# Crossbar transposes for more heads of an attention kernel, with three staging buffers and two crossbar targets

## The chip, the cores and the metric

The kernel runs on one core of one Trainium2 chip. The metric is the device time of one execution in microseconds; the profile's span, from the first to the last instruction, is a little shorter. Three runs of the kernel before took 318.65 to 319.55 us, with a median of 319.01 us.

## The reference

There are two stages. The first is attention over 8 batches, 8 heads, 576 positions and a head dimension of 64. The first four heads see a plain causal window of 32 positions, the last four every fourth position of a causal window of 128:

```python
scores = scale * np.matmul(q, k.transpose(0, 1, 3, 2))
mask_plain = (rel >= 0) & (rel < window)                       # window 32
mask_dil = (rel >= 0) & (rel < window * dilation) & (rel % dilation == 0)   # dilation 4
attn = softmax(where(mask, scores, -1e9))                      # written shorter here
x = (attn @ v), heads side by side: 4608 tokens of 512 features
h = np.maximum(x @ w_in, 0.0)
out = h * h @ w_out
```

The second stage is a feed-forward block with a hidden width of 2048 on the 4608 tokens. Inputs and output are 32-bit floats; the kernel computes in bf16.

## The kernel before, in words

**Two interleaved streams.** TensorE runs the feed-forward block in groups: tiles of 512 tokens (the first four of 256), each of 16 or 8 groups of first-layer matmuls (line 529; the Relu is on ScalarE at line 540, the square on VectorE at line 541) and 16 or 8 groups of second-layer matmuls (line 561). Between the groups stand the steps of the attention of later batches, so that a batch's rows of xT are ready when the feed-forward block reaches them. The schedule is manual: each engine runs its instructions in the order in which the program names them, and waits on semaphores where data or a buffer is not ready.

**The order** is written out in the string PROGRAM for batches 0 to 4 and the loads of 5 and 6, and by a rule (dictionaries LOAD_V, CROSS, LOAD_QK and attention_steps) after that. A bar closes a feed-forward group. Heads are taken in four pairs: pairs 0 and 1 are the plain ("near") heads, 2 and 3 the dilated ones. A code such as 3k1 means batch 3, step k, pair 1. The steps are: q and k (capitals for a second part), which bring a pair's q or k into its transposed layout; v and V, which spread v; a and b, the scores of the two halves with exponential and mask (function scores); o and p, the products with v and the division (function pv). Codes that begin with L are loads: L2:qw0123 loads q and k of batch 2 whole, L4:q10123 those of part 1 of batch 4, L2:vwpdr its v, and L4:x issues batch 4's crossbar transposes.

**Two ways to transpose.** q and k come from HBM with the positions on the partitions and are needed with the head dimension there. GpSimd's DMA queue loads them, cast to bf16, into the staging buffers rb, of which there are two, used by batches in turn. In batches 0 to 3, function trans transposes on TensorE: for a pair of heads 8 transposes (line 265) into a PSUM tile, from which VectorE, or for q of the near pairs ScalarE, copies into qT or the block-diagonal kbd (function halves, lines 278 to 298). From batch 4 on (XB = 4), function cross issues four DMA transposes on SyncE's queue (line 217), one each for q and k and for the two parts of 64 and 80 rows, from the staging buffer into one pair of SBUF tiles, qx and kx; VectorE copies from these. Batches 2 and 3 (WHOLE) are staged in another layout, in which one load brings a whole tensor as 72 rows twice.

**Queues.** GpSimd issues all loads in program order, SyncE all stores of the output (line 504) and the crossbar transposes, also in order. A load into a staging buffer waits until the transposes of the batch that used it before have read it; a crossbar transpose waits until its target's last reader is done.

Of the kernel before, what the change touches and what calls it, by code (L numbers as in the profile page):

```python
# [12 lines left out]
RES = 4  # L13
# [5 lines left out]


PROGRAM = (
    "L0:q023 L0:q00 L0:q01 0k0 L0:q10123 0q0 0q1 0k1 L0:v0pd 0a0 0q2 L0:i0 0a1 0k3 L0:v1dpr 0k2 0q3 0Q1 "
    "0K3 0a3 0Q3 0K2 0a2 0v2 0Q0 L0:i1 L0:o2 0K0 0o0 0v3 0b0 0Q2 0o2 0K1 0b3 0o1 L0:o0 0o3 0V3 0b2 0b1 | "
    "0V2 | 0p0 | 0p1 0p2 | L0:o1 0p3 L0:o3 | | | y | | | | | | | | L1:q00123 z | | | | | L1:v0dp "
    "L1:q10123 | | L2:qw0123 L1:v1dpr 1q1 1q3 | 1q2 | 1k2 | 1k1 1v3 | 1a2 | 1v2 1k0 1q0 | 1o2 | 1a0 1a1 | "
    "1k3 1o0 1o1 | 1a3 1Q0 | 1K0 1o3 | 1Q1 1K1 | 1Q2 | 1b0 | | 1Q3 1K2 L2:vwpdr | | | 2q0 | | 2k0 1V2 | "
    "1b2 1p0 | 1b1 1V3 1K3 | | 1p2 1p1 | 2a0 1b3 | 2k1 2o0 2b0 1p3 | 2q1 2k2 | | L3:qw0123 2q2 2p0 "
    "L3:vwpdr 2a1 | | | 2b1 | 2v2 2o1 2q3 2a2 | | 2p1 | 2k3 | 2b2 2o2 | 2v3 | 2a3 2p2 L4:q10123 | 2b3 | "
    "3k1 2o3 3q1 | | 3a1 L4:q00123 2p3 | 3k0 3k2 | | 3o1 | | | 3q0 3v2 | | | | 3a0 | 3b1 3k3 | | | 3p1 "
    "L4:x 3q2 | | 3b0 | 3a2 3q3 3o0 4k0 | | | 3o2 3b2 | | 3p0 3v3 | 4q1 3a3 | 3p2 4q2 4q0 | L5:q10123 3b3 "  # L30
    "| 3o3 L4:vwpdr | 4k1 | | L5:q00123 3p3 4k2 4k3 4a0 L5:vwpdr | | | 4b0 | | 4q3 | | 4o0 | | | 4a2 4v2 "
    "| 4b2 | 4a3 L5:x 4a1 | 4o2 | | | 4p2 L6:q00123 4v3 | | 4b1 | | 4p0 | | 4p1 | 5q0 5k0 | 4b3 | | | | "
    "4o1 | | 5k2 L6:q10123 4o3 | 5q2 5k1 | | 4p3 | 5q1 |"
)


# [24 lines left out]
def kernel(  # L61
# [9 lines left out]
    nc = tc.nc  # L71
    P = nc.NUM_PARTITIONS
    B, H, S, D = q.shape
# [3 lines left out]
    bf16 = mybir.dt.bfloat16  # L77
# [5 lines left out]
    NE = H // 2  # L83
# [3 lines left out]
    M = S // RES  # L87
    MS = (0, 64)
    MN = (64, M - 64)
    NT = 512  # L90
    NTILES = NTOK // NT
    XB = 4
    WHOLE = tuple(range(2, XB))
    PARTED = (0, 1)
    ADDED = 4
    RING = 4 * S
# [3 lines left out]
    const = ctx.enter_context(tc.tile_pool(name="const", bufs=1))  # L100
# [26 lines left out]
    ]  # L127
    w_out_sb = const.tile([P, NF, DM], bf16, name="w_out_sb")
    xT = const.tile([P, KT, RING], bf16, name="xT")
    rb = [{nm: const.tile([80, 2 * H * RES * D], bf16, name=f"{nm}b{i}") for nm in "qk"} for i in range(2)]  # L130
    qT = const.tile([P, NE, RES, M], bf16, name="qT")

    qx = const.tile([P, H, 2, M], bf16, name="qx")
    kx = const.tile([P, H, 2, M], bf16, name="kx")
    kbd = const.tile([P, NE, NB, P], bf16, name="kbd")
    vbd = [const.tile([P, NE, NB, P], bf16, name=f"vbd{i}") for i in range(2)]

# [5 lines left out]
    def staged(b: int, nm: str):  # L143


        t = rb[b % 2][nm]
        if b in WHOLE:
            return t[:, :].rearrange("p (h a x) -> p h a x", h=H, a=2)
        return t[:, :].rearrange("p (a h x) -> p a h x", h=H, a=2)

    def load_qk(b: int, part, es):
        hs = slice(2 * es[0], 2 * es[-1] + 2)
        for nm, src in (("q", q), ("k", k)):
            t = staged(b, nm)
            if b in WHOLE:
                nc.gpsimd.dma_start(
                    t[0 : M // 2, hs, :, :].rearrange("p h a x -> p (h a) x"),
                    src[b, hs, :, :].rearrange("h (a p r) d -> p (h a) (r d)", a=2, r=RES),
                )
            else:  # L160
                t0, n = RES * MS[part], MN[part]
                nc.gpsimd.dma_start(  # L162
                    t[0:n, part, hs, :], src[b, hs, t0 : t0 + RES * n, :].rearrange("h (p r) d -> p h (r d)", r=RES)
                )

    def load_v(b: int, parts, which="pdr"):

# [35 lines left out]
    def spread_v(b: int, e: int, parts):  # L203

        p0, p1 = parts[0], parts[-1] + 1
        for hl in range(2):
            rows = slice(64 * hl, 64 * hl + 64)
            nc.vector.tensor_copy(
                vbd[b % 2][rows, e, RES * p0 : RES * p1, rows],
                vds[b][rows, e - NE // 2, p0:p1, :].rearrange("p m (r d) -> p (m r) d", d=D),  # L210
            )


    def cross(b: int, nm: str, part: int):

        n, m0 = MN[part], MS[part]
        nc.sync.dma_start_transpose(
            (qx if nm == "q" else kx)[:, :, :, m0 : m0 + n].rearrange("p h c m -> p (h c) m"),
            staged(b, nm)[0:n, part, :, :].rearrange("p h x -> p (h x)"),
        )  # L220

    def trans(b: int, e: int, nm: str, part: int):

        ps = ps_a.tile([P, 1024], bf16, name="pa")
        t = staged(b, nm)
        copy = nc.scalar.copy if nm == "q" and e < NE // 2 else nc.vector.tensor_copy
        if b == 0:

            m0, n = MS[part], MN[part]
            pv_ = ps[:, 0 : RES * n].rearrange("p (r m) -> p r m", r=RES)  # L230
            for r in range(RES):
                for hl in range(2):
                    nc.tensor.transpose(  # L233
                        pv_[64 * hl : 64 * hl + 64, r, :],
                        t[0:n, part, 2 * e + hl, D * r : D * r + D],
                        ident[0:n, 0:n],
                    )
            if nm == "q":
                copy(qT[:, e, :, m0 : m0 + n], pv_)
                return  # L240
            for hl in range(2):
                rows = slice(64 * hl, 64 * hl + 64)
                if e < NE // 2:
                    copy(  # L244
                        kbd[rows, e, m0 // 16 : (m0 + n) // 16, rows].rearrange("p i (m r) -> p i m r", r=RES),
                        pv_[rows, :, :].rearrange("p r (i m) -> p i m r", m=16),
                    )
                else:
                    copy(kbd[rows, e, RES * part : RES * part + RES, rows], pv_[rows, :, 0:64])  # L249
                    if part:  # L250
                        copy(
                            kbd[rows, e, 8, rows].rearrange("p (m r) -> p m r", r=RES),
                            pv_[rows, :, 64:n].rearrange("p r m -> p m r"),
                        )
            return
        if b in WHOLE:
            m0, n, pitch, cuts = 0, M, M, [(t[0:72, :, a, :], 72 * a, 72) for a in range(2)]
        else:

            m0, n, pitch, cuts = MS[part], MN[part], 80, [(t[0:80, part, :, :], 0, 80)]  # L260
        pv_ = ps[:, 0 : 4 * pitch].rearrange("p (h c m) -> p h c m", h=2, c=2)
        for hl in range(2):
            for c in range(2):
                for src, c0, w in cuts:
                    nc.tensor.transpose(  # L265
                        pv_[:, hl, c, c0 : c0 + w], src[:, 2 * e + hl, P * c : P * c + P], ident[0:w, 0:w]
                    )
        halves(e, nm, pv_[:, :, :, 0:n], m0, n, copy)
# [193 lines left out]
    def step(b: int, code: str):  # L462

        what, e = code[0], int(code[1])
        part = int(what in "QKVbp")
        if what in "qk" and b >= XB:
            t = qx if what == "q" else kx
            halves(e, what, t[:, 2 * e : 2 * e + 2, :, :], 0, M, nc.vector.tensor_copy)  # L470
        elif what in "qQkK":
            trans(b, e, what.lower(), part)
        elif what in "vV":
            spread_v(b, e, [part] if b in PARTED else [0, 1])
        elif what in "ab":
            scores(b, e, part, *((ps_f, "pf") if b == 0 and not part else ()))
        elif b == 0 and part and e % 2:
            pv(b, e, part, ps_a, "pa")
        elif b in PARTED and e % 2:
            pv(b, e, part, ps_f, "pf")  # L480
        else:
            pv(b, e, part)
# [135 lines left out]
    def cross_all(b):  # L618
        for part in range(2):
            for nm in "kq":  # L620
                cross(b, nm, part)
# [42 lines left out]
    for g, group in enumerate(groups):  # L664
        for b in [x for x in CROSS if CROSS[x] == g]:
            cross_all(b)
        for b in [x for x in LOAD_V if LOAD_V[x] == g]:
            load_v(b, [0, 1])
        for b in [x for x in LOAD_QK if LOAD_QK[x] == g]:
            for part in range(2):  # L670
                load_qk(b, part, [0, 1, 2, 3])
        group()
        for code in program[g + 1] if g + 1 < len(program) else ():
            run(code)
        while steps and steps[0][0] <= g:
            step(*steps.pop(0)[1:])
# [30 lines left out]
```

The softmax here doesn't subtract the row's maximum and nothing guards it: scores larger than these inputs give would overflow.

## Time and profile before

| what | value |
|---|---|
| time, median of three | 319.01 us |
| span of the profiled run | 317.3 us, TensorE clock 1.000 |
| TensorE busy | 299.7 us (94%) |
| VectorE, ScalarE busy | 208.6 us (66%), 195.4 us (62%) |
| TensorE transposes of line 265 | 192, from 45.1 to 115.7 us |
| crossbar transposes of line 217 | 16, from 100.1 to 207.7 us |
| a crossbar transpose, issue to landing | 3.6 to 11.4 us, median 4.4 |

The profile is one execution, taken by the hardware profiler. PE is TensorE's matmuls, PEld its weight loads, which overlap them, DVE is VectorE, ACT ScalarE, POOL GpSimd, and SPq SyncE's queue. A row of groups names the line, the engine, the operation and its tiles, then busy time and mean duration of one in ns, then the engine's idle time before it. In a time line the columns are start and duration in us. The mean of a matmul contains its latency; neighbours overlap, so what one costs TensorE is read from the distance between starts. "DMA share" of a stretch is the mean share of the 16 DMA engines in which packets were under way; with two queues it can pass 1.

### The profile page before, as it was taken

How to read it: one execution, taken by the hardware profiler on the slowest of the kernel's cores; microseconds unless marked ns; L12 is line 12 of the kernel's file. 1: busy time of each engine (PE TensorE's matmuls, PEld its weight loads, DVE VectorE, ACT ScalarE, POOL GpSimd, SP SyncE). 2: the span in 40 equal slices, each digit the busy share in tenths (PEclk: the TensorE clock that was granted, in tenths of full speed). 3: DMA queues.
4: the chain of work that ended last, by engine and by line, in shares of the span. 5: the costliest groups of instructions: out<-in, count | busy, mean ns of one | idle time of the engine just before them, and what ended most of it. 6: DMA issues, size and time to landing. Idle time of an engine off the chain costs nothing.

```text
span 317.3 us, 6743 instructions
## 1 busy us (share of the span) xinstructions
PE 299.7 (94%) x2523; PEld 190.3 (60%) x2556; DVE 208.6 (66%) x664; ACT 195.4 (62%) x422; POOL 84.1 (27%) x130
## 2 busy tenths in 40 slices
PE   1698999999999999999999999999999999999995
PEld 1587945877965555555579755555555555445543
DVE  6785758898987987996599658965896324204400
ACT  5366735877958966686468646864686466316511
POOL 8762282367320037741271041000000000000000
PEclk9999999999999999999999999999999999999999
DMA  7999999999996619999699864352200210021022
GB/s 96 179 123 212 207 144 204 130 91 162 108 119 130 120 16 204 159 186 167 91 132 174 134 99 90 49 103 68 66 2 2 68 66 0 24 78 33 0 68 66
DMA packets 73056, 33.08 MB, mean 104 GB/s; under 512 B 44096, under 2 KB 67008, under 8 KB 73024
## 3 DMA queue, kind: packets, MB, share of 16 engines
q0 software_dynamic: 48096, 18.36, 50.3%
q1 hardware_dynamic: 24784, 14.16, 19.0%
q8 instruction: 20, 0.33, 0.4%
q10 hardware_dynamic: 144, 0.13, 0.1%
q14 instruction: 12, 0.10, 0.1%
HBM read 36.83 MB, written 9.44 MB: 146 GB/s over the span
## 4 chain that ended last, share of the span: by engine, by line
PE 88%; DVE 5%; ACT 3%; issue 2%; DMA 1%; POOL 1%; ACTq 0%; DVEq 0%; POOLq 0%
PE pf L529 38%; PE pf L561 37%; PE po L443 3%; PE pd L445 3%; PE pa L265 2%; PE pa L334 2%; PE pa L340 1%; DMA kb<-in_k_dram 1%; DVE xT L458 1%; PE pa L233 1%; DVE kbd L244 1%; DVE kbd L249 1%; ACT rec L447 1%; ACT qT L278 1%; ACT rec L448 1%
## 5 line engine op out<-in xcount | busy, mean ns | idle before, releaser
L529 PE MATMUL pf<-xT,w_in 128*128 128x256 bf16 (+1 forms) x758 | 132.9, 325 | 1.2 <-DVE xT L458 0.3
L561 PE MATMUL pf<-w_out_sb,h2T 128*128 128x512 bf16 (+1 forms) x569 | 131.0, 373 | 1.7 <-ACT osb L567 0.5
L529 PEld LDWEIGHTS <-w_in 128*128 128x128 bf16 x768 | 82.1, 114 | 35.7 <-issue 1.3
L540 ACT ACTIVATE h2T<-pf 128x512 bf16<-128x512 f32 x144 | 83.4, 597 | 24.7 <-PE pf L529 23.8
L561 PEld LDWEIGHTS <-h2T 128*128 128x128 bf16 x592 | 54.2, 98 | 53.5 <-issue 0.7
L541 DVE TENSOR_TENSOR h2T<-h2T 128x512 bf16<-128x512 bf16 x144 | 57.3, 422 | 36.0 <-ACT h2T L540 34.8
L567 ACT COPY osb<-pf 128x512 f32<-128x512 f32 (+1 forms) x37 | 21.2, 573 | 44.5 <-PE pf L561 41.5
L458 DVE TENSOR_TENSOR xT<-po,rec 128x288 bf16<-128x288 f32 (+2 forms) x56 | 25.5, 456 | 34.8 <-ACT rec L448 34.2
L447 ACT ACTIVATE rec<-pd 128x288 f32<-128x288 f32 (+2 forms) x56 | 23.1, 412 | 28.1 <-PE pd L445 28.0
L179 POOL DMA_DIRECT2D vbd<-in_v_dram x40 | 28.2, 728 | 43.8 <-PE pd L445 34.6
L344 ACT ACTIVATE pt<-pa 128x352 bf16<-128x352 f32 (+6 forms) x60 | 29.7, 502 | 8.4 <-PE pa L340 4.4
L448 ACT ACTIVATE rec<-rec 128x256 f32<-128x256 f32 (+2 forms) x64 | 28.4, 444 | 2.0
L443 PEld LDWEIGHTS <-vbd 128*128 128x128 bf16 x332 | 19.6, 99 | 10.2 <-issue 1.4
L443 PE MATMUL po<-pt,vbd 128*128 128x32 bf16 (+3 forms) x286 | 19.6, 199 | 0.7 <-DVE xT L458 0.7
L445 PE MATMUL pd<-pt,mk 128*128 128x96 bf16 (+5 forms) x172 | 18.0, 207 | 0.0
L162 POOL DMA_DIRECT2D qb<-in_q_dram x14 | 10.1, 721 | 27.0 <-PE po L443 24.6
L192 POOL DMA_DIRECT2D vd<-in_v_dram x24 | 14.7, 648 | 9.6 <-DMA kb<-in_k_dram 9.6
L278 DVE COPY qT<-qx 64x288 bf16<-64x288 bf16 x64 | 16.1, 251 | 0.8
L282 DVE COPY kbd<-kx 64x288 bf16<-64x288 bf16 x32 | 15.0, 469 | 0.4
L198 POOL DMA_DIRECT2D vbd<-in_v_dram x16 | 9.7, 617 | 17.4 <-PE pd L445 5.1
L334 PE MATMUL pa<-qT,kbd 128*128 128x96 bf16 (+2 forms) x160 | 13.8, 206 | 0.5 <-DVE kbd L244 0.4
L445 PEld LDWEIGHTS <-mk 128*128 128x128 bf16 x232 | 13.7, 99 | 0.7 <-issue 0.5
(60 smaller groups left out, 231.0 us busy)
## 6 DMA issues: line engine op xcount, KB each, us to landing
out_dram<-osb SPq DMA_DIRECT2D x18, 128.0 KB, 4.8
vd<-in_v_dram POOLq DMA_DIRECT2D x32, 64.0 KB, 5.2
w_in<-in_moe_w_in_dram POOLq DMA_DIRECT2D x2, 1024.0 KB, 9.0
w_out_sb<-in_moe_w_out_dram POOLq DMA_DIRECT2D x4, 512.0 KB, 13.5
qb<-in_q_dram POOLq DMA_DIRECT2D x6, 320.0 KB, 5.1
kb<-in_k_dram POOLq DMA_DIRECT2D x6, 320.0 KB, 6.6
vbd<-in_v_dram POOLq DMA_DIRECT2D x24, 72.0 KB, 5.8
out_dram<-osb SPq DMA_DIRECT2D x10, 160.0 KB, 2.2
```

Of the source, the lines that this page charges most:

```text
L179: nc.gpsimd.dma_start(dst[rows, e, i0:i1, rows], v[b, 2 * e + hl, 64 * i0 : 64 * i1, :].rearrange("(i p) d -> p i d", p=64),)
L344: nc.scalar.activation(pt[:, off : off + n], ps[:, 0:n], ACT.Exp, scale=SCALE)
L443: nc.tensor.matmul(oo, vb[:, e, i, :], rh, start=(x == 0), stop=(x == len(mms) - 1), skip_group_check=True)
L445: nc.tensor.matmul(dd, ones[:, :], rh, start=(x == 0), stop=(x == len(dms) - 1), skip_group_check=True)
L447: nc.scalar.activation(rec[:, 0:n], d[:, 0:n], ACT.Ln)
L448: nc.scalar.activation(rec[:, 0:n], rec[:, 0:n], ACT.Exp, scale=-1.0)
L458: nc.vector.tensor_tensor(out=tok, in0=o if o is o3 else o[:, 0:n], in1=rec if o is o3 else rec[:, 0:n], op=ALU.mult)
L529: nc.tensor.matmul(acc[u][:, nt * x + y0 : nt * x + y1], w_in_sb[piece][:, kt, c0 : c0 + 509 : 4], xT[:, kt, t0 : t0 + y1 - y0], start=(kt ...
L540: nc.scalar.activation(hv, acc[u][:, :].rearrange("p (x n) -> p x n", x=per), ACT.Relu)
L541: nc.vector.tensor_tensor(out=hv, in0=hv, in1=hv, op=ALU.mult)
L561: nc.tensor.matmul(cur[m][:, c0:c1], h2[:, f, P * m : P * m + P], w_out_sb[:, f, c0:c1], start=(f == 0), stop=(f == NF - 1),)
L567: nc.scalar.copy(osb[:, c0:c1], cur[m][:, c0:c1])
```

## The change

Crossbar transposes begin with the dilated heads of batch 2 and all heads of batch 3, in place of batch 4. Batches 2 and 3 lose their own staging layout and are loaded in two parts, as the others are. The near heads of batch 2 still go over TensorE, now from the two parts of 64 and 80 rows. There are three staging buffers in place of two, so a batch's loads no longer wait for the batch two before it but for the one three before, and two pairs of crossbar targets in place of one, so that a batch's crossbar transposes need not wait for the copies of the batch before. q of the near heads of batch 3 is copied by ScalarE, as before, but out of SBUF. The purpose is to take transposes off TensorE and to give loads and transposes room.

In the order, L2:x comes one group after batch 2's v loads, batch 3's q and k loads move ahead to the same place, and L3:x follows 2k2. All other codes keep their places.

```diff
-L1:q10123 | | L2:qw0123 L1:v1dpr 1q1 1q3 | 1q2 | ...
+L1:q10123 | | L2:q00123 L2:q10123 L1:v1dpr 1q1 1q3 | 1q2 | ...
-1Q0 | 1K0 1o3 | 1Q1 1K1 | 1Q2 | 1b0 | | 1Q3 1K2 L2:vwpdr | | | 2q0 | | 2k0 1V2 |
+1Q0 | 1K0 1o3 | 1Q1 1K1 | 1Q2 | 1b0 | | 1Q3 1K2 L2:vwpdr L3:q00123 L3:q10123 | L2:x | | 2q0 | | 2k0 1V2 |
-2a0 1b3 | 2k1 2o0 2b0 1p3 | 2q1 2k2 | | L3:qw0123 2q2 2p0 L3:vwpdr 2a1 |
+2a0 1b3 | 2k1 2o0 2b0 1p3 | 2q1 2k2 L3:x | | 2q2 2p0 L3:vwpdr 2a1 |
...
-    XB = 4
-    WHOLE = tuple(range(2, XB))
+    XB = 2
...
-    rb = [{nm: const.tile([80, 2 * H * RES * D], bf16, name=f"{nm}b{i}") for nm in "qk"} for i in range(2)]
+    rb = [{nm: const.tile([80, 2 * H * RES * D], bf16, name=f"{nm}b{i}") for nm in "qk"} for i in range(3)]
...
-    qx = const.tile([P, H, 2, M], bf16, name="qx")
-    kx = const.tile([P, H, 2, M], bf16, name="kx")
+    qx = [const.tile([P, H, 2, M], bf16, name=f"qx{i}") for i in range(2)]
+    kx = [const.tile([P, H, 2, M], bf16, name=f"kx{i}") for i in range(2)]
...
-        t = rb[b % 2][nm]
-        if b in WHOLE:
-            return t[:, :].rearrange("p (h a x) -> p h a x", h=H, a=2)
+        t = rb[b % 3][nm]
...
-        n, m0 = MN[part], MS[part]
+        n, m0, h0 = MN[part], MS[part], H // 2 if b == XB else 0
         nc.sync.dma_start_transpose(
-            (qx if nm == "q" else kx)[:, :, :, m0 : m0 + n].rearrange("p h c m -> p (h c) m"),
-            staged(b, nm)[0:n, part, :, :].rearrange("p h x -> p (h x)"),
+            (qx if nm == "q" else kx)[b % 2][:, h0:, :, m0 : m0 + n].rearrange("p h c m -> p (h c) m"),
+            staged(b, nm)[0:n, part, h0:, :].rearrange("p h x -> p (h x)"),
         )
...
-        if b in WHOLE:
-            m0, n, pitch, cuts = 0, M, M, [(t[0:72, :, a, :], 72 * a, 72) for a in range(2)]
+        if b == 2:
+            m0, n, pitch, cuts = 0, M, M, [(t[0 : MN[a], a, :, :], MS[a], MN[a]) for a in range(2)]
...
-        if what in "qk" and b >= XB:
-            t = qx if what == "q" else kx
-            halves(e, what, t[:, 2 * e : 2 * e + 2, :, :], 0, M, nc.vector.tensor_copy)
+        if what in "qk" and (b > XB or b == XB and e >= NE // 2):
+            t = (qx if what == "q" else kx)[b % 2]
+            by_act = what == "q" and e < NE // 2 and b < ADDED
+            halves(
+                e, what, t[:, 2 * e : 2 * e + 2, :, :], 0, M, nc.scalar.copy if by_act else nc.vector.tensor_copy
+            )
```

## The prediction

> **What bounds the kernel now.** I read the page first, then the busy time by stretch, the waits of each engine, and the time lines of TensorE and of SyncE's queue where the change lies. Page, busy time and DMA row in 40 slices of 7.9 us:
>
> ```profile
> PE 299.7 (94%) x2523; PEld 190.3 (60%) x2556; DVE 208.6 (66%) x664; ACT 195.4 (62%) x422; POOL 84.1 (27%) x130
> ...
> DMA  7999999999996619999699864352200210021022
> ```
>
> TensorE has the work. DMA looks full up to 95 us, then shows a hole (6, 6, 1) from 95 to 119 us. Busy time of the engines by stretch (PE, PEld, DVE, ACT, POOL, granted clock, DMA share, GB/s):
>
> ```profile
> 66.00:79.00 13.00, 12.84 (x176) 9.12 (x176) 11.67 (x40) 9.65 (x23) 8.30 (x12) 1.00 1.06 129
> 79.00:97.00 18.00, 17.79 (x209) 13.64 (x211) 16.09 (x53) 14.02 (x34) 4.59 (x7) 1.00 0.99 125
> 97.00:118.00 21.00, 20.80 (x185) 12.41 (x187) 17.44 (x57) 16.75 (x37) 1.79 (x3) 1.00 0.41 77
> ```
>
> These stretches hold all transposes that the change removes, and TensorE is busy in 51.4 of their 52 us. In the waits of TensorE there is nothing of size: 0.2 us for a transpose's target, 0.3 to 0.7 us elsewhere, after a 6.4 us start. So TensorE time taken out here is time off the end, unless a new wait replaces it. The DMA share passes 1 where two queues overlap, and the bytes differ much at a full row (77 to 221 GB/s), so a 9 is not a proof of saturation.
>
> [...] a batch's q and k, 1,180 KB, took 9.9 us (119 GB/s) on a quiet DMA. [...] a crossbar transpose beside loads took 11.4 us and alone 4.4. [...]
>
> **What is removed.** Batch 2 loses pairs 2 and 3, batch 3 all four, for q and k: 4 + 8 = 12 calls of trans, each of 8 TensorE transposes (two heads, two halves, two cuts), 96 in all. TensorE's time line:
>
> ```profile
> 78.30 0.42 PE L265 MATMUL pa<-mk,qb 72*128 72x72 bf16 x8
> 78.56 0.43 PE L265 MATMUL pa<-mk,kb 72*128 72x72 bf16 x8
> 78.82 1.94 PE L529 MATMUL pf<-xT,w_in 128*128 128x256 bf16 x16
> ```
>
> The latencies overlap, so I take the starts: 78.30, 78.56, 78.82, or 0.26 us for eight. Twelve times 0.26 is 3.1 us. The weight loads lie inside this pitch. Batch 2's pairs 0 and 1 keep their transposes, cut 64 + 80 in place of 72 + 72: the same 144 columns, nothing.
>
> **The copies** stay on their engines; only the source changes:
>
> ```profile
> L278 DVE COPY qT<-qx 64x288 bf16<-64x288 bf16 x64 | 16.1, 251 | 0.8
> L278 DVE COPY qT<-pa 64x288 bf16<-64x288 bf16 x16 | 4.9, 304 | 0.2
> ```
>
> For q of the dilated pairs of two batches: 16 x (304 - 251) = 0.8 us. For k of the same pairs 16 x (287 - 230) = 0.9, and near k 8 x (480 - 469) = 0.1. VectorE gains 1.8 us. ScalarE keeps batch 3's near q (391 ns from PSUM; from SBUF not shown; I take the same, and bound it by a third more, 8 x 0.13 = 1.0 us of ScalarE, beside TensorE's work).
>
> **What is added.** Four crossbar transposes of half size for batch 2, four whole ones for batch 3, all on SyncE's queue. The four loads of two whole batches become eight: four more issues of 0.7 us on GpSimd, which sits idle longer than that. Batch 3's k is issued after q without the 2.8 us wait for batch 1's transposes, since the third buffer takes batch 2. The price of a crossbar batch, quiet (batch 4) and beside loads (batch 5), in SyncE's time line:
>
> ```profile
> 100.13 1.34 SPq L217 DMA_TRANSPOSE kx<-kb  x1
> ...
> 103.52 1.99 SPq L217 DMA_TRANSPOSE kx<-kb  x1
> 105.61 1.97 SPq L217 DMA_TRANSPOSE qx<-qb  x1
> ...
> 133.78 1.24 SPq L217 DMA_TRANSPOSE kx<-kb  x1
> ...
> 138.66 6.21 SPq L217 DMA_TRANSPOSE kx<-kb  x1
> 144.97 3.75 SPq L217 DMA_TRANSPOSE qx<-qb  x1
> ```
>
> The last ones land 4.4 and 5.8 us after their issue. Quiet: 100.1 to 110.0, the last two 6.5 us. Contended: 133.8 to 150.8, the last two 12.1 us.
>
> **Does batch 2's land in time?** Its loads land at 53.9 and 59.0 in the trace (issues at 43.3 and 44.3, landing after 10.6 and 14.7 us). SyncE is free after its store at 59.6. Half the bytes: estimate 5 to 9 us, so 65 to 69 us. First use, 2k2, is at 78.6 us: 9 us of slack. Free.
>
> **Does batch 3's?** Its first use is 3k1, then 3q1, and TensorE's 3a1 waits for both. Time line of before:
>
> ```profile
> 95.05 2.01 DVE L282 COPY kbd<-pa 64x288 bf16<-64x288 bf16 x4 [0.29 <-PE pa L265]
> ...
> 96.19 1.59 ACT L278 COPY qT<-pa 64x288 bf16<-64x288 bf16 x4
> ...
> 97.84 0.32 PE L334 MATMUL pa<-qT,kbd 128*128 128x96 bf16 x4
> ```
>
> ScalarE ends at 97.78 and TensorE starts at 97.84: no slack there. Six of the twelve removed calls stand before 3a1, or 1.6 us, so all four must have landed by about 96.2 - 1.6 = 94.6. Before, batch 3's k was issued at 71.3 and landed 12.6 us later, at 83.9. Its second part now is issued at some 70, but shares the DMA with the first two transposes, which SyncE reaches at 77: I keep 84. Then two transposes remain: 84 + 6.5 = 90.5 quiet, 84 + 12.1 = 96.1 contended. Beside them run batch 3's v until 88 and then batch 4's loads. The middle is 93.3, just in time, so I cost it at zero; the bound from above is 1.5 us. Behind the waiting VectorE copies stand the squares and masks, behind ScalarE's the Relus.
>
> **Batch 4's** loads landed at 98.2 and its first copy came at 118.3. The added crossbar work delays the loads by up to 3.5 us; batch 5's loads, which waited 24.6 us until 116.2 for a staging buffer, now come near 92 and compete. The need is then at 118.3 - 3.1 = 115.2. Quiet, they are there at 98.2 + 3.5 + 9.9 = 111.6; contended at 101.7 + 17 = 118.7, though k alone is needed first, which the contended case had 1.2 us sooner: 2.3 us late at worst, in the middle 114.6 and not late; I take zero. After that the hole at 103 to 119 us is used, two targets end waits of 6.3 us on SyncE, and nothing there holds TensorE.
>
> **Forecast:** 319.0 - 3.1 = 315.9; I add 0.2 for the copies that move closer together: 316.1.
>
> **Rivals.** (a) Batch 3's transposes land contended: 1.5 us given back, 317.6. For it: L4's loads are no longer held 2.7 us by batch 2's transposes, so they press sooner; against: half of that stretch has only v, in front of which batch 5's first transpose took 5.8 us. (b) The crossbar is starved twice: k's last part lands at 88 and the pair takes 12.1 us, 100.1 or 5.5 us late: 319.0 - 3.1 + 5.5 = 321.4, slower. For it: in batch 5 the loads all landed before the second transpose did; against: the even cut and the earlier issue. (c) VectorE becomes the bound: it is busy 45.2 of 52 us now, 43.4 of 48.9 then (89%). If its chains set the pace, the 3.1 us turn into idle time: 319.0, no change. For it: few idle gaps; against: TensorE hardly waits for it now.
>
> **Chances.** Forecast 0.5, (a) 0.2, (b) 0.18, (c) 0.12. Faster by over 0.3% means under 318.05: the first two, 0.70. Within: (c), 0.12. Slower: 0.18. Low end: no 0.2 and TensorE's few waits (0.4 to 0.7 us) gone too, 315.2. The high end takes in (a) and (c) and leaves most of (b) out: 319.8.
>
> **What would show it.** Line 265 with 192 - 96 = 96 transposes, and about 3.1 us less busy TensorE; no new wait in TensorE's list from 90 to 120 us; batch 3's last crossbar landing by 94 us; batch 5's first load near 92 us instead of 116. Wrong if VectorE or ScalarE show waits for a crossbar landing, TensorE a wait for kbd or qT, or if the sum of these exceeds 3 us. Stores piling up behind a waiting SyncE would show as ScalarE's output copy waiting for a store.

## The result, and the profile after

The changed kernel is slower: 327.41 us (325.93 to 329.05) against 319.03 us, a ratio of 1.0262 with a 95% interval of 1.0221 to 1.0303. The forecast was 316.1 us. The profile is of the slowest of its four executions (329.05 us). The mean granted clocks of the four are 0.989, 0.987, 0.995 and 0.994, so the four differ in how long the clock was low. From its page, the span, the busy time, the granted clock and the DMA:

```profile
span 327.3 us, 6600 instructions
...
PE 304.9 (93%) x2460; PEld 189.7 (58%) x2460; DVE 207.2 (63%) x664; ACT 195.7 (60%) x422; POOL 85.6 (26%) x134
...
PEclk9999999999999699999999999999999999999999
DMA  7999999999999991999469987731210120031021
```

Ninety-six transposes are gone, and yet TensorE is busy for 5.2 us longer. One slice, the fourteenth (106 to 115 us), has a granted clock of 0.6. The hole in the DMA row has moved: the loads and transposes run on to 121 us without a break. Between 85 and 125 us the waits of TensorE are these two, in total and longest; before, that stretch had none of this list:

```profile
PE pa L325 <- ACT qT L269: 6.2, 1, 6.2
PE po L434 <- DVE xT L449: 0.6, 1, 0.6
```

Line 325 is a score matmul, here 3a1, the place that the prediction named. TensorE's time line there, and ScalarE's copy before it (3q1):

```profile
99.00 1.46 PE L523 MATMUL pf<-xT,w_in 128*128 128x512 bf16 x6
106.65 0.45 PE L325 MATMUL pa<-qT,kbd 128*128 128x96 bf16 x4 [6.19 <-ACT qT L269]
106.91 0.51 PE L434 MATMUL po<-pt,vbd 128*128 128x96 bf16 x5
107.26 0.48 PE L436 MATMUL pd<-pt,mk 128*128 128x192 bf16 x3
107.58 4.43 PE L523 MATMUL pf<-xT,w_in 128*128 128x512 bf16 x10
```
```profile
104.84 1.75 ACT L269 COPY qT<-qx 64x288 bf16<-64x288 bf16 x4 [5.63 <-DMA qx<-qb]
```

ScalarE has waited for qx, a crossbar landing, until 104.84. Ten first-layer matmuls then take 4.43 us; 16 took 3.62 us before. That is the clock, 0.50 here and 1.00 there: 0.44 us for one against 0.23. Busy time by stretch has it in the third column from the right:

```profile
105.00:110.00 5.00, 3.35 (x18) 1.76 (x18) 1.61 (x4) 3.40 (x8) 2.42 (x5) 0.53 1.22 148
110.00:115.00 5.00, 5.00 (x26) 2.54 (x25) 4.52 (x18) 3.84 (x8) 0.27 (x1) 0.79 1.33 146
```

The low clock goes with the 6.2 us gap: in stretches of half a microsecond the clock is 1.00 up to 105.0 us, 0.81 in the next, 0.50 from 105.5 to 112.0 and 0.86 in the one after. By these means it steps down at 105.3 us, 4.9 us after TensorE had run out of work, and up at 112.1. A gap of 3.7 us in experiment 1 left it at 1.00. From 3a1 to the score matmuls that follow (106.65 to 118.33) TensorE took 11.7 us, and 9.5 us in the same stretch of run 2 below, which has no such gap (100.73 to 110.20): the slow clock costs 2.2 us on top of the wait.

Why is the landing late? SyncE's queue with batch 3's crossbar transposes, and GpSimd's queue with the loads of batches 4 and 5:

```profile
79.89 1.39 SPq L208 DMA_TRANSPOSE kx<-kb  x1
81.39 2.23 SPq L208 DMA_TRANSPOSE qx<-qb  x1
83.71 6.74 SPq L208 DMA_TRANSPOSE kx<-kb  x1
90.55 6.45 SPq L208 DMA_TRANSPOSE qx<-qb  x1
```
```profile
81.33 0.76 POOL L153 DMA_DIRECT2D qb<-in_q_dram  x1
82.05 0.75 POOL L153 DMA_DIRECT2D kb<-in_k_dram  x1
82.76 0.72 POOL L153 DMA_DIRECT2D qb<-in_q_dram  x1
83.44 0.72 POOL L153 DMA_DIRECT2D kb<-in_k_dram  x1
84.11 0.78 POOL L153 DMA_DIRECT2D qb<-in_q_dram  x1
84.82 0.78 POOL L153 DMA_DIRECT2D kb<-in_k_dram  x1
```

The four transposes are issued one after another from 79.9 us. Batch 3's loads were in time: the last, issued at 70.42, landed after 7.7 us, at 78.1. From 81.3 to 84.8 us, beside and just after the second transpose, six loads with 1,792 KB are issued on the other queue. The four transposes land 5.5, 13.9, 16.6 and 14.2 us after their issue, the last at 104.8: 24.9 us for what took 9.9 us on a quiet DMA. Part of it shows in the issue itself: the third and fourth occupy SyncE's queue for 6.7 and 6.5 us.

A second loss is in TensorE's own row, at batch 2's near heads:

```profile
66.33 1.15 PE L256 MATMUL pa<-mk,qb 64*128 64x64 bf16 x8
67.31 1.90 PE L555 MATMUL pf<-w_out_sb,h2T 128*128 128x512 bf16 x8
69.14 1.17 PE L256 MATMUL pa<-mk,kb 64*128 64x64 bf16 x8
70.13 1.04 PE L555 MATMUL pf<-w_out_sb,h2T 128*128 128x512 bf16 x4
```

The row shows the form of the first of the eight; four have 64 rows and four have 80, in turn. The start of the next work is 0.98 and 0.99 us later, where eight transposes of 72 rows took 0.26. The trace names the rows of each (`64*128`, `80*128`), not why a change between them takes time.

There are seven changes of size inside a call; if they are what costs, that is 0.72 / 7 = 0.10 us each, by estimate. The step from the matmuls of 128 rows into the first transpose of 64 costs as much here, and stands ahead of the call. From twelve first-layer matmuls to the transpose after them, before and after:

```profile
76.99 1.48 PE L529 MATMUL pf<-xT,w_in 128*128 128x256 bf16 x12
78.30 0.42 PE L265 MATMUL pa<-mk,qb 72*128 72x72 bf16 x8
```
```profile
79.92 1.48 PE L523 MATMUL pf<-xT,w_in 128*128 128x256 bf16 x12
81.33 1.17 PE L256 MATMUL pa<-mk,qb 64*128 64x64 bf16 x8
```

This is 1.31 us before and 1.41 after. Three of the four calls have this 0.10; the first, which stands 2.79 us behind its 24 matmuls before and 2.80 after, doesn't. The four calls therefore lose 4 x 0.72 + 3 x 0.10 = 3.2 us. Steps between 80 and 128 rows show no such cost: four transposes of 80 rows ahead of a first-layer matmul take 0.14 us (59.67 to 59.81). The experiments test the change of size.

### The profile page after: what moved, and what is told of

Read it like the earlier page. It is cut to its first block, busy times and chain, and to the rows that moved or that the text cites. A ratio compares the mean times of both kernels' runs of the same rounds, so it can differ in the third digit from the quotient of the medians.

```text
span 327.3 us, 6600 instructions
## 1 busy us (share of the span) xinstructions
PE 304.9 (93%) x2460; PEld 189.7 (58%) x2460; DVE 207.2 (63%) x664; ACT 195.7 (60%) x422; POOL 85.6 (26%) x134
## 4 chain that ended last, share of the span: by engine, by line
PE 87%; ACT 4%; DMA 3%; DVE 3%; issue 1%; POOL 1%; SPq 0%; ACTq 0%; DVEq 0%; POOLq 0%
PE pf L523 37%; PE pf L555 37%; PE po L434 3%; PE pd L436 3%; DMA out_dram<-osb 2%; PE pa L256 2%; PE pa L325 2%; PE pa L331 2%; ACT qT L269 1%; PE pa L224 1%; DMA kb<-in_k_dram 1%; DVE xT L449 1%; ACT rec L438 1%; DVE h2T L535 1%; ACT rec L439 1%
## 5 line engine op out<-in xcount | busy, mean ns | idle before, releaser
L523 PE MATMUL pf<-xT,w_in 128*128 128x256 bf16 (+1 forms) x768 | 136.7, 331 | 0.6 <-DVE xT L449 0.3
L555 PE MATMUL pf<-w_out_sb,h2T 128*128 128x512 bf16 (+1 forms) x592 | 134.7, 373 | 0.5 <-ACT osb L561 0.5
L170 POOL DMA_DIRECT2D vbd<-in_v_dram x40 | 28.3, 723 | 87.1 <-PE pd L436 66.8
L269 DVE COPY qT<-qx 64x288 bf16<-64x288 bf16 x80 | 20.3, 253 | 1.1
L273 DVE COPY kbd<-kx 64x288 bf16<-64x288 bf16 x40 | 18.8, 469 | 3.0 <-DMA kx<-kb 2.5
L325 PEld LDWEIGHTS <-kbd 128*128 128x128 bf16 x168 | 10.8, 102 | 10.6 <-issue 4.1
L336 DVE TENSOR_TENSOR pt<-pt,mask_p 128x352 bf16<-128x352 bf16 (+3 forms) x32 | 11.9, 371 | 6.2 <-ACT pt L335 6.0
```

Of the source, the lines that this page charges most:

```text
L170: nc.gpsimd.dma_start(dst[rows, e, i0:i1, rows], v[b, 2 * e + hl, 64 * i0 : 64 * i1, :].rearrange("(i p) d -> p i d", p=64),)
L325: nc.tensor.matmul(ps[:, n : n + w].rearrange("p (r m) -> p r m", r=RES), kbd[:, e, i, :], qT[:, e, :, m0:m1], start=True, stop=True,)
L523: nc.tensor.matmul(acc[u][:, nt * x + y0 : nt * x + y1], w_in_sb[piece][:, kt, c0 : c0 + 509 : 4], xT[:, kt, t0 : t0 + y1 - y0], start=(kt ...
L555: nc.tensor.matmul(cur[m][:, c0:c1], h2[:, f, P * m : P * m + P], w_out_sb[:, f, c0:c1], start=(f == 0), stop=(f == NF - 1),)
```

## The experiments

**Theories.** A: the crossbar transposes of batch 3 are starved by loads that now come early. B: they are late because SyncE reaches them late. C: VectorE and ScalarE set the pace, so TensorE time taken out comes back as idle time. D: the early loads hurt by themselves. E: changes between 64 and 80 rows cost TensorE time (the expectations below count eight in a call, at 0.09 us). F: those calls were slow because of DMA traffic into their buffers.

The start-up varies from run to run (the first 24 first-layer matmuls take 3.06 to 4.18 us, in both kinds of kernel), so where a fraction of a microsecond matters I also compare the time from a fixed point, the twelve first-layer matmuls at 59.29 us in the trace of before, to the end: 258.0 us before, 267.5 after.

**1. Batch 4's v ahead of batch 5's first loads.**

```diff
-L5:q10123 3b3 | 3o3 L4:vwpdr |
+L4:vwpdr L5:q10123 3b3 | 3o3 |
```

> The changed kernel with batch 4's v loads put ahead of batch 5's first q and k loads in the order, so that the latter no longer follow batch 4's q and k within a few us but wait behind loads that are held by batch 2's products. Theory A (the crossbar transposes of batch 3 are starved by the loads of batches 4 and 5 that now come early): batch 5's 640 KB drop out of the stretch from 84 to 104 us, batch 3's last crossbar transpose lands some 4 to 5 us sooner (near 100 us), TensorE's wait at 3a1 falls from 6.2 to 1 to 2 us, time 319 to 323 us. Rival B (the crossbar transposes are late because SyncE reaches them late, behind the stores, whatever else runs): landing at 104 us as before, 327 us.

Measured: 323.72 us, ratio 1.0121 (1.0070 to 1.0172). Batch 5's loads move to 107 us, the wait at 3a1 falls to 3.7 us, and the clock stays at 1.00. A wait of 3.7 us therefore did not lower the clock in the profiled execution, one of 6.2 us did; that is no threshold, since one of the four executions of this run has a mean clock of 0.994. The total is better than the change by 3.7 us for 2.5 us of wait; from the fixed point the gain is 4.8 us, which the wait (2.5) and the clock (2.2) make up. This speaks for A, and against B, since SyncE reached the transposes 1.4 us later than in the change (81.27). The last landed at 102.7, where I expected some 100; my estimate of the wait that is left was too low by half. Without batch 5's first loads beside them the four transposes still took 21.4 us (81.3 to 102.7), where they took 9.9 on a quiet DMA.

**2. Batch 4's q and k held behind part of its v,** and batch 5's behind the rest, as in experiment 1.

```diff
-2a3 2p2 L4:q10123 | 2b3 |
+2a3 2p2 L4:vwp L4:q10123 | 2b3 |
...
-L5:q10123 3b3 | 3o3 L4:vwpdr |
+L4:vwdr L5:q10123 3b3 | 3o3 |
```

> The changed kernel with the near-head part of batch 4's v loads put ahead of batch 4's q and k loads, which are then held until batch 2's products have read their v (third such load issued at 91.6 us, fourth at 96.5 us). Theory A: batch 3's crossbar transposes run on a quiet DMA from 80 to about 91 us, no wait at 3a1, TensorE gains the 3.1 us; batch 4's loads land near 107 us and its crossbar transposes come late, which may give back 0 to 4 us: 316 to 320 us. Rival B: 327 us, with the wait at 3a1.

Measured: 321.01 us, ratio 1.0051 (1.0032 to 1.0070). SyncE's queue and TensorE's waits from 85 to 125 us:

```profile
79.60 1.55 SPq L208 DMA_TRANSPOSE kx<-kb  x1
81.26 3.96 SPq L208 DMA_TRANSPOSE qx<-qb  x1
85.31 2.62 SPq L208 DMA_TRANSPOSE kx<-kb  x1
88.03 2.74 SPq L208 DMA_TRANSPOSE qx<-qb  x1
```
```profile
PE pa L325 <- ACT qT L269: 0.4, 1, 0.4
PE po L434 <- DVE xT L449: 0.4, 1, 0.4
PE pf L523 <- DVE xT L449: 0.3, 1, 0.3
```

SyncE issues them at the same time as in the change, and they land at 94.2 (88.03 + 6.2) in place of 104.8. B is out. The wait is gone, and batch 4's later crossbar transposes hold nobody. But the kernel is still slower than before, and 1 us above the range that I expected under A: A alone does not explain the loss.

**3. Batch 3's loads and crossbar transposes early.**

```diff
-L2:vwpdr L3:q00123 L3:q10123 | L2:x |
+L3:q00123 L3:q10123 L2:vwpdr | L2:x L3:x |
...
-2q1 2k2 L3:x |
+2q1 2k2 |
```

> The changed kernel with batch 3's q and k loads ahead of batch 2's v loads, and batch 3's crossbar transposes right after batch 2's, ahead of the four stores of 73 to 80 us on SyncE's queue. Theory A: they land by about 80 us, before batch 4's loads begin (81 us), so nothing waits at 3a1: 316.1 us, the forecast of the prediction, unless batch 4's crossbar transposes are late. Rival B expects the same here. Rival C (VectorE and ScalarE set the pace, so that TensorE time taken out comes back as idle time): 319 us, with TensorE idle by some 3 us more between 66 and 118 us.

Measured: 321.26 us, ratio 1.0055 (1.0033 to 1.0076). The transposes land by 86.6 us and the wait at 3a1 is 0.4 us. From the fixed point runs 2 and 3 both take some 259.7 us, 1.7 more than before, in two different ways of removing the stall. A alone would have given 316.1 us. TensorE is not idle by 3 us more: small waits make up 1.1 to 1.5 us, and the four slow calls 3.2. Against the 3.1 us removed that leaves 0.2 to 0.4 us open. So C is not the cause of the main part, and E became the question.

**4. Three staging buffers and nothing else.**

```diff
-    rb = [{nm: const.tile([80, 2 * H * RES * D], bf16, name=f"{nm}b{i}") for nm in "qk"} for i in range(2)]
+    rb = [{nm: const.tile([80, 2 * H * RES * D], bf16, name=f"{nm}b{i}") for nm in "qk"} for i in range(3)]
...
-        t = rb[b % 2][nm]
+        t = rb[b % 3][nm]
```

> The kernel before with three staging buffers in place of two and nothing else: batches 0 to 3 keep their transposes on TensorE. Theory A: the early loads alone hurt nothing before 100 us, since no crossbar transposes run beside them there; batch 4's transposes meet batch 5's loads, but have 8 us of slack: 319.0 us, within 0.5. Rival D (the early loads hurt by themselves, by holding up v loads or stores): 321 us or more.

Measured: 319.28 us, ratio 0.9999 (0.9983 to 1.0015), with 258.0 us from the fixed point. D is out: without crossbar work beside them the early loads cost nothing that these figures show. Batch 4's four loads and batch 5's first two start here from 83.3 to 89.5 us and land 4.8 to 8.5 us after their issue; in the change, beside the crossbar transposes, the same six took 9.7 to 19.4 us. In the kernel before, batch 4's four loads, also without crossbar transposes beside them, took 4.5 to 7.3 us, and in the change 9.7 to 16.0. So here each slowed the other: the transposes took 24.9 us beside these loads and 9.9 on a quiet DMA.

**5. Alternating cuts on the kernel before.** Batches 2 and 3 are staged in parts, and their transposes, all still on TensorE, are cut as the change cuts batch 2's. The loads in parts are not printed here.

```diff
-            m0, n, pitch, cuts = 0, M, M, [(t[0:72, :, a, :], 72 * a, 72) for a in range(2)]
+            m0, n, pitch, cuts = 0, M, M, [(t[0 : MN[a], a, :, :], MS[a], MN[a]) for a in range(2)]
```

> The kernel before, all transposes of batches 0 to 3 still on TensorE, no crossbar work added, two staging buffers; only batches 2 and 3 are staged in parts and their transposes are cut 64 + 80 rows in turn in place of 72 + 72, as the change does for batch 2's near heads. Theory E (TensorE pays about 90 ns whenever a transpose of 64 rows follows one of 80 or the reverse, so eight of them take 0.98 us where eight of one size take 0.26): sixteen calls by 0.72 us, +11.5 us, 330 to 331 us. Rival F (the four slow calls in the changed kernel were slowed by the DMA traffic into the same buffers): 319.5 us.

Measured: 332.45 us, ratio 1.0403 (1.0379 to 1.0426): 13.1 us more without a single crossbar transpose added. This is 1.5 us above the expected range, because the expectation left out the step into the call: in 15 of the 16 calls the first transpose starts 0.10 us later behind the matmuls ahead of it than before. TensorE's time line has the same pitch for a call as in the change:

```profile
66.74 1.15 PE L263 MATMUL pa<-mk,qb 64*128 64x64 bf16 x8
67.72 1.90 PE L559 MATMUL pf<-w_out_sb,h2T 128*128 128x512 bf16 x7
```

**6. The same, with the rows of one size together.**

```diff
-        for hl in range(2):
-            for c in range(2):
-                for src, c0, w in cuts:
+        for src, c0, w in cuts:
+            for hl in range(2):
+                for c in range(2):
```

> As the run with alternating cuts on the kernel before, but in each call the four transposes of 64 rows come first and then the four of 80. Theory E: two switches in place of eight, some 0.18 us a call over 0.26, +3 us: 322 us. If it is the 64-row transposes that are slow by themselves, whatever stands before them: no gain over alternating, 330 us.

Measured: 322.50 us, ratio 1.0093 (1.0071 to 1.0114).

```profile
66.62 0.53 PE L263 MATMUL pa<-mk,qb 64*128 64x64 bf16 x8
66.97 1.89 PE L559 MATMUL pf<-w_out_sb,h2T 128*128 128x512 bf16 x7
```

The same instructions in another order take 0.35 to 0.37 us a call in place of 0.98. Sixteen calls by 0.62 us are 9.9 us, and the two runs differ by 9.95. So it is the change of size that costs, and F and the slow 64 rows are out. One change is left inside a call, and 0.26 + 0.10 is 0.36. With the step into the call, 16 calls should cost 13.0 us over before in run 5 and 3.2 in run 6; the medians say 13.1 and 3.2, the times from the fixed point 12.7 and 2.6.

**7 and 8. Early or held, with batch 2's cuts padded to 80 rows.** The 16 rows of padding are zeroed once; their columns are overwritten by the second cut.

```diff
-            m0, n, pitch, cuts = 0, M, M, [(t[0 : MN[a], a, :, :], MS[a], MN[a]) for a in range(2)]
+            m0, n, pitch, cuts = 0, M, M, [(t[0:80, a, :, :], MS[a], 80) for a in range(2)]
...
                 nc.vector.memset(staged(1, nm)[64:80, 0, :, :], 0.0)
+                nc.vector.memset(staged(2, nm)[64:80, 0, 0 : H // 2, :], 0.0)
```

> Batch 3's loads and crossbar transposes early (as in the run of that name), and batch 2's near heads transposed as two cuts of 80 rows, the first with 16 zero rows whose columns the second overwrites; two small zeroings on VectorE at 34 us. Theory E with A: four calls by 0.72 us, or 2.9 us, come off 321.3: 318.4 us. Rival C (VectorE and ScalarE set the pace): 321 us still, with waits of TensorE for them in place of the slow transposes.

> Batch 4's loads held (as in the run of that name), and batch 2's near heads transposed as two cuts of 80 rows. Theory E with A: 321.0 less 2.9 is 318.1 us, unless TensorE now reaches 3a1 before batch 3's crossbar transposes have landed (94 us); then up to 2.9 us comes back as a wait there. Rival C: 321 us.

Measured: 318.73 us, ratio 0.9985 (0.9959 to 1.0010), and 318.10 us, ratio 0.9963 (0.9952 to 0.9974). Against the runs without padding that is 2.5 and 2.9 us less; from the fixed point it is 3.4 and 3.1. The first is not different from before; the second, at 0.4% under before, beats both kernels. From its page, and TensorE at batch 2's near heads:

```profile
PE 298.3 (94%) x2428; PEld 187.9 (59%) x2460; DVE 208.2 (66%) x666; ACT 195.1 (62%) x422; POOL 85.6 (27%) x134
```
```profile
66.92 0.45 PE L256 MATMUL pa<-mk,qb 80*128 80x80 bf16 x8
67.20 1.89 PE L555 MATMUL pf<-w_out_sb,h2T 128*128 128x512 bf16 x7
```

A call is back to 0.28 us, and the order of the two sources is still alternating, so it is not the change of source that cost. From the fixed point to the end the kernel takes 256.5 us, 1.5 less than before; three small waits near 3a1 (0.3, 0.5 and 0.3 us) keep 1.1 of the 3.1 us.

**9. The changed kernel with the padded cuts of runs 7 and 8 alone.**

> The changed kernel with nothing altered but batch 2's near transposes, now two cuts of 80 rows. Theory A with E: the landing of batch 3's crossbar transposes is set by the loads and stays near 104.8 us, so the 2.9 us that TensorE saves turn into a longer wait at 3a1 (6.2 to about 9 us): 326 to 328 us, no gain. If the two losses simply add: 324.5 us.

Measured: 325.14 us, ratio 1.0181 (1.0162 to 1.0200). My expectation missed: the losses nearly add. SyncE issues the last crossbar transpose at 87.1 us in place of 90.6, and it lands after 14.8 us at 101.9. So the landing was not fixed by the loads. TensorE now runs some 3 us earlier and with it the stores that stand ahead of the transposes on SyncE; that this is the reason is argued, not tested. The wait at 3a1 is 5.5 us. The clock is low here too: 0.84 on average from 100 to 105 us and 0.82 from 105 to 110, against 1.00 and 0.53 in the change. Estimated from these means, with 0.50 as the low clock, that is from 103.4 to 106.8 us, beginning 5.1 us after TensorE ran out of work and half as long as in the change; the stretch from 3a1 to the next scores takes 10.4 us, 1.0 more than in run 2.

**10 and 11. 3q1 and 3k1 earlier,** on runs 7 and 8.

```diff
-L4:q10123 | 2b3 | 3k1 2o3 3q1 | | 3a1
+L4:q10123 3q1 | 2b3 3k1 | 2o3 | | 3a1
```

> Early loads and crossbar transposes for batch 3 and padded cuts for batch 2, and now 3q1 and 3k1 one to two groups earlier, since nothing on TensorE has to run before them any more. The three small waits of TensorE near 3a1 (0.34, 0.45, 0.27 us in the padded runs) fall away at least in part: 317.6 to 318.2 us, against 318.7 without the move. If VectorE and ScalarE set the pace there (rival C in the small), the waits only change place and 318.7 us stays.

> The same move of 3q1 and 3k1 on the run with batch 4's loads held and padded cuts. Batch 3's crossbar transposes land near 93 us there, and ScalarE now asks for them at about 93: 317.2 to 317.8 us if they are in time, 318 or more if ScalarE waits for them.

Measured: 319.14 us, ratio 0.9997 (0.9983 to 1.0012), and 318.99 us, ratio 0.9992 (0.9979 to 1.0006). A miss: no better than without the move, the second even worse. TensorE's wait at 3a1 is now for kbd, in run 11:

```profile
PE pa L325 <- DVE kbd L273: 1.0, 1, 1.0
PE po L434 <- DVE xT L449: 0.5, 2, 0.3
PE pf L523 <- DVE xT L449: 0.2, 1, 0.2
```

The move put ScalarE's copy 3q1 (1.74 us) ahead of the exponential of 2b3. VectorE waits 1.7 us for that exponential, to apply its mask, and starts the copies of 3k1 at 96.08 us, against 95.49 in run 8, although run 11 is 0.9 us ahead of run 8 at the fixed point. Near 3a1, the chains on VectorE and ScalarE do set the pace by about 1 us. That is rival C in the small.

## Why the prediction was wrong

- **"TensorE has the work", and 3.1 us for the twelve calls: held.** In run 8, with the stall and the changes of size removed, 1.5 us of it (counted from the fixed point) comes off the end and 1.1 us stays as small waits. Of the 0.5 us that remains, the padded calls take 0.1; the rest is not settled.
- **"The same 144 columns, nothing": wrong, and worth 3.2 us.** I counted columns and not changes of size. Four calls, each longer by 0.72 us (0.98 less 0.26), and three steps into them by 0.10 cancel the twelve by 0.26. Runs 5, 6 and 8 show it. The hint was in the kernel before, which pads parts to 80 rows and cuts a whole batch into two equal 72s.
- **Batch 3's transposes "just in time, so I cost it at zero", with 1.5 us as the bound from above: this step failed most.** The place, the instruction and the mechanism were right, the size was not: the last landed at 104.8, not 93.3. The load part of the sum was too late (84 against 78.1) and the transpose part far too short: 24.9 us for the four, where my contended price was 17 us. Batch 5's case, from which I took that price, had fewer loads beside it. In the change, batch 4's four loads and batch 5's first two come together, since the third buffer frees them from a wait. I had each of these arrivals in the text ("press sooner", "come near 92"), batch 5's too late (84.1 us in the trace), and set none beside batch 3's transposes as bytes: 1,792 KB. Of the 10.2 us by which the landing missed the 94.6 us that I had called for, TensorE, itself 4.2 us later at 3a1 than I assumed, hid about four; the wait of 6.2 us is the rest.
- **The clock: not in the prediction.** A wait was costed at its length. This one cost 2.2 us more.
- **Rival (b), "starved twice", was the nearest**, in kind and sign, with 321.4 us and 0.18. Its parts did not come true: its first starvation, batch 3's last load landing at 88, did not happen (78.1), and the second was far larger: the last two transposes took 21.1 us, not 12.1. That its 5.5 us of lateness is close to the 6.2 us of wait is luck, and the changes of size and the clock, which carry the time to 327, are not in it.
- **A crossbar transpose beside loads, 11.4 us against 4.4 alone: held in kind.** The loads are slowed too, from 4.8 to 8.5 us in run 4 to 9.7 to 19.4 in the change. How the DMA engines share their time, these figures do not show.
- **Batch 2's crossbar transposes, free: held.** Issued from 60.2 to 64.3, the last landed after 6.5 us at 70.8, ahead of the use at about 82.
- **Rival (c), no gain because VectorE binds:** wrong for the whole, right for about 1 us, as runs 10 and 11 show.

The sum from the fixed point: 258.0 - 3.1 + 3.2 + 6.2 + 2.2 + 0.6 (the wait for xT) = 267.1, against 267.5 measured. The profiled execution reaches the fixed point 0.5 us later than before.

## What to carry to other kernels

When work moves from a full engine to the DMA queues, list what else will be in flight at that moment, in bytes and after the change, above all loads that the same change frees from a wait; here the order in which the queues issue was worth 6.4 us (the change against run 2), the work removed 3.1. Holding the next loads until the transposes were through turned a stall of 6.2 us into one of 0.4, and a third buffer cost nothing by itself (run 4, ratio 0.9999), where no crossbar transposes ran beside its early loads. Count TensorE's small transposes by their changes between 64 rows and 80 or 128, not by columns: here padding 64 rows to 80 removed 3.1 us, and grouping by size brought a call from 0.98 us to 0.36. And a copy that may now go earlier can still do harm, if it stands ahead of work that another engine waits for: run 11 took 318.99 us, run 8 318.10.

## What was not expected of the hardware

- A step between 64 and 80 rows cost TensorE about 0.10 us (estimated: 0.72 us over seven steps, in the change), and so did one from a matmul of 128 rows to a transpose of 64 (1.41 us against 1.31 for the twelve matmuls ahead). Between 80 rows and 128 no such cost shows: four transposes of 80 rows took 0.14 us (the change), and the same twelve matmuls ahead of one 1.31 (run 8). Eight transposes in turn took 0.98 us (the change, run 5), grouped 0.35 to 0.37 (run 6), padded to one size 0.28 (run 8).
- A gap of 3.7 us at 3a1 (run 1) left the granted clock at 1.00 in the profiled execution. After the gap of 6.2 us (the change) it was 0.50 for 6.8 us, from 4.9 us after TensorE had run out of work; after that of 5.5 us (run 9) the means of 0.84 and 0.82 over five microseconds each give an estimate of 3.4 us at 0.50.
- Beside 1,792 KB of queued loads, three of four crossbar transposes landed 13.9 to 16.6 us after their issue; alone, in the kernel before, they took 3.9 to 4.6. The loads gave way too: they took 9.7 to 19.4 us in place of the 4.8 to 8.5 of run 4.
